# One padded load for the last chunk of W_down, and x in six loads instead of four, in a decode layer on one core

## The chip, the cores and the metric

The kernel runs on one core of one Trainium2 chip. A core has five engines that run their own instruction streams: TensorE (PE: matmuls; PEld: its weight loads), VectorE (DVE), ScalarE (ACT), GpSimd (POOL) and SyncE (SP). Data come from device memory by sixteen DMA engines. A load is issued by SP or by ACT into that issuer's queue, and each of the DMA engines works on its share of the rows. The metric is the device time of one execution in microseconds. Before the change three runs gave 659.60, 659.35 and 658.97; the median is 659.35.

## The reference, cut to what matters

Two tokens (B = 2, one position each) go through a pre-norm attention layer with a key and value cache, and then through a gated feed-forward layer:

```
h  = x + A(layernorm(x))        A: q = n @ wq, 32 heads of 128, 8192 cached positions,
                                   softmax(q k / sqrt(128)) v, then @ wo
h2 = h + Bf(layernorm(h))       Bf: gate = n @ W_gate ; up = n @ W_up
                                    (relu(gate) * up) @ W_down
x [2,1,512]  k_cache, v_cache [2,32,8192,128]  wq [512,4096]  wo [4096,512]
W_gate, W_up [512,1376]  W_down [1376,512]      all bf16
```

The caches make up 268 MB of the 281 MB that are read.

## The kernel before, in words

**The three big buffers.** `bufs[0..2]` hold 64 KB in each of 128 partitions (`TILE` = 32768 bf16 elements). The attention goes through 15 steps of four heads (`steps[0..LASTQ]`, "quad" steps) and two last steps of two heads (p0, p1). The K tile of a quad step is 8 MB and fills one buffer; the V tile is as large. The three buffers are used in turn, in the order K0, V0, K1, V1, K2, ...; a load can only be issued when the tile that was in its buffer has been used up. The V tile of step 1 takes K0's buffer, and goes out when step 0's scores are done; the K tile of step 2 takes V0's buffer, and goes out when step 0's values are done. `bufs[2]` holds wq (4 MB), the row of q and x before K1.

**Order of the work.** All is written out by hand inside `tc.manual_schedule()`: every engine runs its instructions in the order in which they stand. The start is: x (L197 to L200, issued by ACT), then wq, K0 and V0 (L201 to L203, issued by SP). x is transposed on TensorE (L246), normalised (`ln_cols`, L177 to L193), multiplied by wq (L260), and the row of q is spread over the partitions into `qrep` (L272) and `qpair` (L279). Only then is K1 issued (L294), since wq and q lie in its buffer. A step then multiplies K with q on VectorE (`products`, L390), adds up in halves (`scores`, L408, L410), takes the exponentials (L430) and multiplies with V on TensorE (`values`, L461); a part of the scores goes over TensorE (`scores_pe`, L355 to L382).

**The loads' completion counters.** Each load, from whichever queue, gets one of eight completion counters in turn, in the order of the program. A load waits on its issuer until the load eight before it, which had the same counter, has landed, besides waiting for its buffer. SP works through its loads in order, so a load that waits holds those behind it.

**The feed-forward layer.** F = 1376 is not a multiple of 128: ten chunks of 128 rows, and an eleventh that begins at row F - 128 = 1248, so that its first 32 rows are rows that chunk ten already has (`AGAIN` = 32, `FSETS`, `FC` = 11). W_down lies in `wd_sb` as 128 x 11 x 512. Before the change the eleventh chunk is loaded without its first 32 partitions, by three loads of 32 rows (L651 to L654), and VectorE writes zeros into those 32 partitions (L684). Then come four loads with chunks 0 to 4, 5 to 7, 8 and 9 (L655 to L657). W_gate and W_up are read in the same chunks, so gate and up values of the 32 repeated rows exist a second time in the eleventh chunk, and meet the zeros in W_down. The gate is made at L745 for all eleven chunks at once; L766 multiplies it with up, first chunks 0 to 4, then 5 to 10. `down` (L756) then takes chunks 0 to 4, the eleventh, and 5 to 9, and two engines copy the sum to `yrow` (L773, L774), which the last load stores (L775).

Of the kernel before, what the change touches and what calls it, by code (L numbers as in the profile page):

```python
# [13 lines left out]
def _free(t, offset, dims):  # L14

    return bass.AP(tensor=t.tensor, offset=t.offset + offset, ap=[t.ap[0]] + [list(d) for d in dims])


def _dram(t, offset, dims):
    return bass.AP(tensor=t.tensor, offset=t.offset + offset, ap=[list(d) for d in dims])  # L20
# [3 lines left out]
def kernel(  # L24
# [13 lines left out]
    nc = tc.nc  # L38
    P = nc.NUM_PARTITIONS
    B, Sq, D = A_x.shape  # L40
    _, Hkv, Sk, Dh = A_k_cache.shape
    Hq = A_wq.shape[1] // Dh
    F = B_W_gate.shape[1]
# [33 lines left out]
    FSETS = [(0, 5), (5 * P, 3), (8 * P, 1), (9 * P, 1), (F - P, 1)]  # L77
    FC = 11
    AGAIN = 32
# [55 lines left out]
    wd_sb = bufs[1][:, 0:FC * D].rearrange("p (c n) -> p c n", c=FC)  # L135
# [58 lines left out]

    with tc.manual_schedule():

        for b, k, n in ((0, 0, 2), (0, 2, 2), (1, 0, 2), (1, 2, 2)):  # L197
            nc.scalar.dma_start(
                out=xr[b:b + 1, k * P:(k + n) * P], in_=_dram(A_x, b * D + k * P, [[D, 1], [1, n * P]]),
            )  # L200
# [9 lines left out]
            out=nscale, in_=nscale, compare_op=ALU.not_equal, fill=-SCALE,  # L210
# [5 lines left out]
            out=ident_f, in_=ident_f, compare_op=ALU.not_equal, fill=1.0,  # L216
# [4 lines left out]
            out=sel, in_=sel, compare_op=ALU.not_equal, fill=1.0,  # L221
# [9 lines left out]
            out=pick, in_=pick, compare_op=ALU.not_equal, fill=1.0,  # L231
# [24 lines left out]
        for g0 in range(0, NQ, 4):  # L256
            for n0 in range(NH * g0 * Dh, NH * (g0 + 4) * Dh, 4 * Dh):
                q_ps = ps2.tile([B, 4 * Dh], f32, tag="o")
                for c in range(KC):
                    nc.tensor.matmul(  # L260
                        out=q_ps, lhsT=xn[:, c, :], rhs=wq_sb[:, c, n0:n0 + 4 * Dh], start=(c == 0), stop=(c == KC - 1),
                    )
                nc.vector.tensor_copy(qrow[:, n0:n0 + 4 * Dh], q_ps)
            for b in range(B):
                r_ps = ps2.tile([P, 4, Dh], f32, tag="tp")
                for j in range(NH):
                    nc.tensor.matmul(
                        out=r_ps[j * (P // NH):(j + 1) * (P // NH)], lhsT=sel[:, b, 0:P // NH],
# [5 lines left out]
        for j in range(2):  # L274
            nc.tensor.matmul(
                out=r_ps[j * (P // 2):(j + 1) * (P // 2)], lhsT=sel[:, B - 1, :],
# [202 lines left out]
        def values_cols(s, t0, t1):  # L479

            if t0 == 0:
                o_ps[s.i] = ps2.tile([P, 8], f32, tag="o", name="o_ps")
            for t in range(t0, t1):
                nc.tensor.matmul(
                    out=o_ps[s.i][:, 0:2], lhsT=s.vt[:, t * Dh:(t + 1) * Dh],
                    rhs=s.pg[:, t // VG, :, t % VG], start=(t == 0), stop=(t == s.nt - 1),
                )
# [133 lines left out]
        for d0, r, k, m in DEALT:  # L621
            for i in range(m):
                n, at_o = k * PORT, 2 * (d0 > 0) * D
                nc.sync.dma_start(
                    out=wdeal[i * SIDE2:i * SIDE2 + n, at_o:at_o + r * D],
                    in_=_dram(A_wo, (HL * Dh + d0 + i * n * r) * D, [[r * D, k], [k * r * D, PORT], [1, r * D]]),
# [20 lines left out]
        for w, src in ((0, B_W_gate), (1, B_W_up)):  # L647
            nc.sync.dma_start(
                out=wgu[:, w].rearrange("p c f -> p (c f)"), in_=_dram(src, 0, [[KC * F, P], [1, KC * F]]),
            )  # L650
        for q0 in range(AGAIN, P, AGAIN):  # L651
            nc.sync.dma_start(
                out=wd_sb[q0:q0 + AGAIN, FC - 1, :], in_=_dram(B_W_down, (F - P + q0) * D, [[D, AGAIN], [1, D]]),
            )  # L654
        for f0, n in FSETS[:-1]:  # L655
            fc = f0 // P
            nc.sync.dma_start(out=wd_sb[:, fc:fc + n, :], in_=_dram(B_W_down, f0 * D, [[n * D, P], [1, n * D]]))  # L657
        late = bufs[1][:, HALF + D:HALF + D + P + D]
        hrow, parts3 = late[0:3 * B, 0:D], late[0:3 * B, D:D + B]
# [6 lines left out]
            out=z2_ps, lhsT=ones, rhs=_free(zc, ((B - 1) * NQ + groups[Q][1]) * NH, [[1, nb]]), start=True, stop=True,  # L666
# [13 lines left out]
        for k, t1 in ((1, 40), (2, 56), (3, 72)):  # L680
            values_cols(p1, t0, t1)
            lay_rows(k, sps[k - 1]) if k < len(SETS) else lay_dealt()
            t0 = t1
        nc.vector.memset(wd_sb[0:AGAIN, FC - 1, :], 0.0)  # L684
        values_cols(p1, 72, 88)
        sums(Q + 2)
        shares(Q + 2)
# [45 lines left out]
        for c in range(KC):  # L733
            nc.tensor.transpose(hT_ps[:, c, :], hb[:, c].rearrange("p k b -> p (k b)"), ident)
        nc.scalar.activation(
            out=hrow.rearrange("q (p c) -> q p c", c=KC), in_=hT_ps.rearrange("q c p -> q p c"), func=ACT.Copy,
# [7 lines left out]
        gate = small.tile([P, FC, B], f32, tag="gate")  # L744
        nc.vector.scalar_tensor_tensor(  # L745
            out=gate, in0=g_ps, scalar=0.0, in1=_free(rvar, 0, [[0, FC], [1, B]]), op0=ALU.max, op1=ALU.mult,
        )
        parts = [(range(0, UP), "of", ps), (range(UP, FC), "tp", ps2)]
        u_ps = [pool.tile([P, len(part), B], f32, tag=tag, name="u_ps") for part, tag, pool in parts]
        SIDE = P // KC  # L750
# [55 lines left out]
```

## Time and profile before

| | |
|---|---|
| median of three runs | 659.35 us |
| profiled execution | 659.72 us |
| its span, first to last instruction | 657.9 us |
| TensorE busy | 351.5 us (53%) |
| VectorE busy | 558.8 us (85%) |
| ScalarE busy | 123.5 us (19%) |
| GpSimd busy | 8.5 us (1%) |
| moved by DMA | 281.37 MB, 428 GB/s on average |
| mean granted TensorE clock | 0.759 |

The span is the time between the first and the last instruction; 1.8 us of the execution lie around it. Busy shares are averages over the whole span. In timeline rows the columns are start, duration (both us), engine, line, operation, operands and, in brackets, how long the engine had been idle and what ended that. In the chain of work they are start, duration and what ran or was waited for. `tile` stands for any of the three buffers. A queue's row gives its packets, megabytes and the share of the sixteen engines' time.

### The profile page before, as it was taken

To read this page: it belongs to the slowest core of one execution; us is meant where nothing else is said; L and a number is where in the kernel's file an instruction comes from. 1 tells how busy PE (TensorE), PEld (TensorE's weight loads), DVE (VectorE), ACT (ScalarE), POOL (GpSimd) and SP (SyncE) were. 2 spreads that over 40 slices of the span, in tenths; PEclk is the share of its full clock that TensorE was granted. 3 is DMA by queue.
4 is the path that set the end of the run, shared out by engine and by line. 5 is a ranking of instruction groups with operands and counts; after the bars stand their busy time and mean duration, and the time that the engine had idled before them with its cause. 6 is when DMAs were issued, how large, how long until landed. Compare 5 with 4: busy or idle time off the path is not lost.

```text
span 657.9 us, 5149 instructions
## 1 busy us (share of the span) xinstructions
PE 351.5 (53%) x2132; PEld 160.4 (24%) x2132; DVE 558.8 (85%) x256; ACT 123.5 (19%) x337; POOL 8.5 (1%) x34
## 2 busy tenths in 40 slices
PE   1730924709175380926538093562908458291997
PEld 0210311304022130312214031220403224030466
DVE  1499697988979799897979989796997969999982
ACT  1130030301103020030302103030210304201870
POOL 2000000000000000000000000000000000000010
PEclk9975876959679595866959587695967869686885
DMA  9999999999999999999999999999999999999997
GB/s 383 446 443 442 390 447 439 442 434 408 442 438 439 434 415 442 430 446 431 418 442 427 442 438 423 442 427 435 442 427 431 434 431 438 434 424 426 420 423 284
DMA packets 6994, 281.37 MB, mean 428 GB/s; under 512 B 790, under 2 KB 1532, under 8 KB 1980
## 3 DMA queue, kind: packets, MB, share of 16 engines
q1 hardware_dynamic: 6964, 281.06, 99.1%
q8 instruction: 16, 0.26, 0.1%
q14 instruction: 6, 0.05, 0.0%
q10 hardware_dynamic: 8, 0.00, 0.0%
HBM read 281.05 MB, written 0.00 MB: 427 GB/s over the span
## 4 chain that ended last, share of the span: by engine, by line
DVE 42%; DMA 37%; PE 18%; ACT 1%; issue 1%; SPq 0%; ACTq 0%; DVEq 0%
DMA tile<-in_A_k_cache_dram 30%; DVE tile L390 19%; DVE tile L408 18%; PE pv_ps L461 16%; DMA tile<-in_A_wo_dram 4%; DVE scol L410 2%; DMA tile<-in_A_x_dram 2%; DMA tile<-in_B_W_down_dram 1%; PE q_ps L260 1%; DVE pgq L435 1%; ACT ecol L430 1%; DVE pm L414 1%; DVE qrep L410 0%; DVE pm L425 0%; DVE hmax L427 0%
## 5 line engine op out<-in xcount | busy, mean ns | idle before, releaser
L461 PE MATMUL pv_ps<-tile,pgq 128*16 128x512 bf16 x960 | 241.5, 417 | 237.2 <-DVE pgq L435 224.8
L390 DVE TENSOR_TENSOR tile<-tile,qrep 128x29696 bf16<-128x29696 bf16 (+3 forms) x16 | 232.4, 14525 | 46.5 <-DMA tile<-in_A_k_cache_dram 46.5
L408 DVE TENSOR_TENSOR tile<-tile 128x14848 bf16<-128x14848 bf16 (+7 forms) x68 | 236.4, 3477 | 2.2
L461 PEld LDWEIGHTS <-pgq 128*16 128x16 bf16 x960 | 91.1, 97 | 376.9 <-DVE pgq L435 235.4
L365 ACT ACTIVATE tile<-t_ps 128x1024 bf16<-128x1024 bf16 x53 | 52.6, 1022 | 16.2 <-PE t_ps L364 15.8
L466 ACT ACTIVATE pv<-pv_ps 16x512 f32<-16x512 f32 (+1 forms) x16 | 9.4, 588 | 240.9 <-PE pv_ps L461 240.9
L430 ACT ACTIVATE ecol<-scol,nmax 128x256 bf16<-128x256 f32 x14 | 7.1, 507 | 197.4 <-DVE nmax L429 197.4
L364 PE MATMUL t_ps<-ident,tile 128*128 128x128 bf16 x424 | 32.6, 230 | 16.4 <-DMA tile<-in_A_k_cache_dram 16.4
L355 PE MATMUL row_ps<-tile,qz 128*24 128x512 bf16 (+1 forms) x98 | 30.6, 394 | 18.3 <-ACT tile L365 18.2
L364 PEld LDWEIGHTS <-tile 128*128 128x128 bf16 x424 | 26.0, 103 | 31.8 <-DMA tile<-in_A_k_cache_dram 17.2
L410 DVE TENSOR_REDUCE scol<-tile 128x232 f32<-128x1856 bf16 (+1 forms) x14 | 28.9, 2067 | 0.5
L435 DVE TENSOR_TENSOR pgq<-ecol,ownb 128x1024 bf16<-128x1024 bf16 x15 | 10.4, 692 | 10.3 <-ACT ecol L430 10.3
L396 ACT ACTIVATE tile<-tile 128x128 bf16<-128x128 bf16 x60 | 17.6, 294 | 1.9 <-DVE tile L390 1.9
L390 DVE TENSOR_TENSOR tile<-tile,qpair 128x4096 bf16<-128x4096 bf16 (+3 forms) x4 | 15.5, 3883 | 0.0
L355 PEld LDWEIGHTS <-qz 128*24 128x24 bf16 (+1 forms) x98 | 7.9, 93 | 28.3 <-issue 23.3
L382 ACT ACTIVATE scol<-sc_ps 32x24 f32<-32x24 f32 (+1 forms) x56 | 11.7, 209 | 7.7 <-PE sc_ps L377 7.2
L377 PE MATMUL sc_ps<-ident_f,tile 24*128 24x24 f32 (+2 forms) x68 | 7.2, 221 | 11.0 <-ACT tile L373 11.0
L373 ACT ACTIVATE tile<-row_ps 24x512 f32<-24x512 f32 (+2 forms) x17 | 9.9, 585 | 13.5 <-PE row_ps L355 13.5
L396 ACT ACTIVATION_READ_ACCUMULATOR tile<-tile 128x1 f32 x60 | 11.2, 187 | 0.0
L377 PEld LDWEIGHTS sc_ps<-ident_f,tile 24*128 24x128 f32 (+2 forms) x68 | 5.5, 136 | 19.4 <-ACT tile L373 19.4
L247 DVE CAST xc<-x_ps 128x8 f32<-128x8 bf16 x1 | 0.2, 167 | 11.3 <-PE x_ps L246 11.3
L260 PE MATMUL q_ps<-tile,xn 128*2 128x512 bf16 x32 | 9.1, 444 | 1.0 <-DVE xn L193 1.0
(141 smaller groups left out, 135.4 us busy)
## 6 DMA issues: line engine op xcount, KB each, us to landing
tile<-in_A_k_cache_dram SPq DMA_DIRECT2D x2, 4096.0 KB
tile<-in_A_v_cache_dram SPq DMA_DIRECT2D x2, 4096.0 KB, 19.9
tile<-in_A_wq_dram SPq DMA_DIRECT2D x1, 4096.0 KB, 12.3
tile<-in_A_wo_dram SPq DMA_DIRECT2D x1, 2048.0 KB, 24.4
tile<-in_B_W_gate_dram SPq DMA_DIRECT2D x1, 1376.0 KB, 18.0
tile<-in_B_W_up_dram SPq DMA_DIRECT2D x1, 1376.0 KB
tile<-in_A_wo_dram SPq DMA_DIRECT2D x1, 1024.0 KB
tile<-in_B_W_down_dram SPq DMA_DIRECT2D x1, 640.0 KB
```

Of the source, the lines that this page charges most:

```text
L260: nc.tensor.matmul(out=q_ps, lhsT=xn[:, c, :], rhs=wq_sb[:, c, n0:n0 + 4 * Dh], start=(c == 0), stop=(c == KC - 1),)
L355: nc.tensor.matmul(out=row_ps, lhsT=z, rhs=s.kt[:, (nv + c0 + k) * Dh:(nv + c0 + k + 4) * Dh], start=(u == 0), stop=(u == U - 1),)
L364: nc.tensor.transpose(t_ps[:, k, :], s.kt[:, t * Dh:(t + 1) * Dh], ident)
L365: nc.scalar.activation(out=s.kt[:, (nv + c0) * Dh:(nv + c0 + TPC) * Dh], in_=t_ps.rearrange("p t s -> p (t s)"), func=ACT.Copy,)
L377: nc.tensor.transpose(sc_ps[:, t].rearrange("p u j -> p (u j)"), rows[:, t * P:(t + 1) * P], ident_f[0:nh * U, 0:nh * U],)
L390: nc.vector.tensor_tensor(out=kv, in0=kv, in1=_free(s.qr, 0, [[0, n], [1, Dh]]), op=ALU.mult)
L396: nc.scalar.activation(out=kv, in_=kv, func=ACT.Copy, accum_out=scols[s.i][:, t:t + 1])
L408: nc.vector.tensor_tensor(out=lo, in0=lo, in1=hi, op=ALU.add)
L410: nc.vector.tensor_reduce(out=scol[:, s.na:s.nv], in_=_free(s.kt, s.na * Dh, [[Dh, s.nv - s.na], [1, 8]]), axis=AXIS.X, op=ALU.add,)
L430: nc.scalar.activation(out=ecol, in_=scols[s.i], func=ACT.Exp, scale=SCALE, bias=nmax, accum_out=zs[:, s.b, s.g:s.g + 1],)
L435: nc.vector.tensor_tensor(out=s.pg, in0=_free(ecol, 0, [[VG, s.nt // VG], [0, NH], [1, VG]]), in1=_free(ownb, 0, [[0, s.nt // VG], [VG, NH ...
L461: nc.tensor.matmul(out=pv_ps[s.i][r, :], lhsT=s.pg[:, u].rearrange("p j t -> p (j t)"), rhs=s.vt[:, u * VG * Dh:(u + 1) * VG * Dh], start= ...
```

## The change

x, which is one row of 512 elements for each of the two tokens, is loaded in six pieces instead of four: for each token one of 256 elements and two of 128 instead of two of 256. The eleventh chunk of W_down is loaded whole, 128 rows in one load, the first of five from the list `FSETS[-1:] + FSETS[:-1]`; its first 32 partitions now hold the rows that chunk ten has too. The zeros are no longer written into W_down but into the gate values of those 32 partitions, after L745. The number of loads in all stays the same (two more for x, two fewer for W_down); 32 KB more are read. In the changed kernel the lines from L652 on have other numbers.

```diff
-        for b, k, n in ((0, 0, 2), (0, 2, 2), (1, 0, 2), (1, 2, 2)):
+        for b, k, n in ((0, 0, 2), (0, 2, 1), (0, 3, 1), (1, 0, 2), (1, 2, 1), (1, 3, 1)):
             nc.scalar.dma_start(
                 out=xr[b:b + 1, k * P:(k + n) * P], in_=_dram(A_x, b * D + k * P, [[D, 1], [1, n * P]]),
             )
...
-        for q0 in range(AGAIN, P, AGAIN):
-            nc.sync.dma_start(
-                out=wd_sb[q0:q0 + AGAIN, FC - 1, :], in_=_dram(B_W_down, (F - P + q0) * D, [[D, AGAIN], [1, D]]),
-            )
-        for f0, n in FSETS[:-1]:
-            fc = f0 // P
+        for f0, n in FSETS[-1:] + FSETS[:-1]:
+            fc = FC - 1 if f0 == F - P else f0 // P
             nc.sync.dma_start(out=wd_sb[:, fc:fc + n, :], in_=_dram(B_W_down, f0 * D, [[n * D, P], [1, n * D]]))
...
-        nc.vector.memset(wd_sb[0:AGAIN, FC - 1, :], 0.0)
...
+        nc.vector.memset(gate[0:AGAIN, FC - 1, :], 0.0)
```

## The prediction

> **What bounds the kernel now.** First the page's head, its forty slices and its queues, to see whether one resource is full throughout:
>
> ```profile
> span 657.9 us, 5149 instructions
> ...
> DMA  9999999999999999999999999999999999999997
> ...
> q1 hardware_dynamic: 6964, 281.06, 99.1%
> ...
> q10 hardware_dynamic: 8, 0.00, 0.0%
> ```
>
> The sixteen DMA engines are busy in every slice but the last. VectorE (85%) often waits for K, TensorE (53%) for VectorE. So the time is 281 MB at what the engines move, plus each stretch in which an engine has nothing queued, plus what follows the last byte. q1 is SP's queue, with every large load; q10 is ACT's, with x alone: four loads, eight packets, so two each (the data, then the completion count). The chain of work that ended last names the places the change touches:
>
> ```profile
> 1.82 10.70 DMA tile<-in_A_x_dram
> ...
> 28.59 43.74 DMA tile<-in_A_k_cache_dram
> ...
> 644.58 9.73 DMA tile<-in_B_W_down_dram
> 654.31 0.04 issue
> 654.35 0.60 PE d_ps L758 x16
> 654.96 0.03 issue
> 654.99 0.33 PE d_ps L758 x4
> ```
>
> 2 KB of x take 10.7 us. The transfer view in a window from 6 to 7 us (forty bins of 25 ns, GB/s of the packets that start in each) shows why:
>
> ```profile
> GB/s 1311 0 1331 2621 1311 0 0 1311 0 2621 0 0 2621 2621 0 0 0 1311 2621 0 0 0 0 0 0 0 1311 0 0 0 0 0 0 0 0 0 0 0 0 0
> DMA packets 17, 0.52 MB, mean 525 GB/s; under 512 B 0, under 2 KB 1, under 8 KB 1
> ...
> q10 hardware_dynamic: 1, 0.00, 0.2%
> ```
>
> 1311 is one 32 KB row of wq; the 20 over it in the third bin is 512 B of x. The same 20 stands at 8.5 and 10.95 us, the small second packets between. After load one (both packets before 2 us), x gets one packet through for each 1.22 us row of wq: 6.06, 7.3, 8.5, 9.75, 10.95 and 12.18 us. TensorE starts on x at 12.66. The timeline then tells how much room the stages have:
>
> ```profile
> 28.59 0.34 SPq L173 DMA_DIRECT2D tile<-in_A_k_cache_dram  x1
> ...
> 32.42 15.09 DVE L390 TENSOR_TENSOR tile<-tile,qrep 128x28672 bf16<-128x28672 bf16 x1 [1.74 <-DMA tile<-in_A_k_cache_dram]
> ...
> 64.48 0.33 SPq L173 DMA_DIRECT2D tile<-in_A_v_cache_dram  x1
> ...
> 72.45 15.63 DVE L390 TENSOR_TENSOR tile<-tile,qrep 128x29696 bf16<-128x29696 bf16 x1 [5.44 <-DMA tile<-in_A_k_cache_dram]
> ```
>
> VectorE was ready for step 0 at 30.68 and waited 1.74 us for K. Step 1's V load is issued at 64.48, when step 0's scores free K's buffer, 32.06 us after step 0's products start. Between the K load of step 1 and that V load nothing else is queued. The packets where the one ends and the other begins, 69.8 to 72.3 us in bins of 62.5 ns:
>
> ```profile
> GB/s 0 0 0 0 0 0 0 4194 4195 3146 2097 1049 0 0 1049 0 0 0 0 0 0 0 0 0 0 0 0 0 0 0 0 0 0 1049 0 0 0 0 0 0
> ```
>
> The first 64 KB rows of V start on 14 engines from 70.24 to 70.5, on one at 70.7, on one at 71.8. Fifteen engines would run dry if that load arrived after about 70.5.
>
> **The change part by part.** *x in six loads.* Twelve packets instead of eight, on the same engine. The first eight fall as before, to 12.18 us. There wq ends: its own count lets packet nine through at once, and ten, eleven and twelve each wait for a row of K, which is 64 KB. From their first starts (12.2 to 12.7) to the count packets (31.1 to 32.0) eight rows take 19.3 us, so 2.41 each. The last packet goes at 12.18 + 3 x 2.41 = 19.4, TensorE starts at 19.9: x is 7.24 us later. Bounds: two rows (4.8 us) if x gets in one turn earlier at the start, four (9.65 us) if wq's last row and its count make one turn. I take three, since x's own counts had turns of their own.
>
> The Trainium skill, page "DMA: Bandwidth & Descriptors", section "Queues, rings and completion order", says that an engine switches between queues only after a whole packet, typically 9 to 17 descriptors. With K's eight rows and count as one packet, x would wait for whole tiles, three times about 19 us. Here wq gave x a turn after each row, so the trace speaks for one row a turn.
>
> What hangs on x (transposes, norm, wq, q's copies) moves whole by 7.24: nothing in it waits for another load, wq having landed at 13.0. Step 1's K load goes out at 28.59 + 7.24 = 35.8, covered by V of step 0, whose rows run to about 51. VectorE is ready at 30.68 + 7.24 = 37.92, so step 0 starts 5.5 us late; 1.74 us of its wait is the cover used up. The V load of step 1 moves to 64.48 + 5.5 = 69.98. From an issue to its first packets the nearest row is wq's at the start: 0.74 to 1.73 us, so 0.99. The rows arrive at 70.97: a gap of 0.27 to 0.73 us on fifteen engines, none on the sixteenth. Refilling costs more: after the start wq's first row was followed by its second after 1.85 us instead of 1.22, 0.63 lost. Loss per engine: from 0 (the late engine decides the end) to 0.73 + 0.63 = 1.36. I take 1.36, because the counts show the late engine changing along the run (at 109 to 111 us two lag, at 553 to 557 all sixteen are spread over 3 us), so the engine that ends last is most likely one that lost.
>
> Next in line is step 2's K load, issued at 82.92 when step 0's values are done: 88.4, its rows at 89.4, while V's rows now end at 89.5 + 1.0 or more: covered. VectorE ends step 0 at 67.01 + 5.5 = 72.5, level with the K it waits for (72.45), so its 5.44 us of idle time is gone but step 1 starts on time, and from step 2 on all is as before, later by the gap. 281 MB at a full rate leave no place to win that back.
>
> *Waits of the loads.* Completion counters go round by eight, so a load waits for the one eight before it. The V load of step 0 now waits on SP for the first x load (both packets out by 2 us): from 1.64 to about 2.5. Behind it on SP is only step 1's K load; 4 + 8 MB stand in the queue until 31 us. Nothing. The two more issues on ACT (213 to 506 ns each) push its table load, which ends at 3.4, by at most 1 us, against x at 19.9. Nothing. Later loads keep the same partners, the total being the same.
>
> *W_down's tail.* Three loads of 32 rows (issues of 0.34, 0.31 and 0.42 us) become one. The last of W_down's loads waited 2.5 us for W_gate and went out at 647.91; it now waits for a piece of W_o that had landed, and goes at about 644.5 before the shift. Each engine gets eight 1 KB rows and one count for six rows and three counts; the packets of 654.0 to 654.5 (34 in 17.4% of 16 engines, 0.5 us) cost 0.041 us each, so the change is 0. By bytes alone 32 KB at 428 GB/s are +0.08, which I take; below, the earlier issue could gain at most 0.4, since the 20 matmuls after 654.35 could then follow the 24 before them without the wait. *Memsets.* Gone is 0.27 us at 642.35, ahead of a wait for TensorE of 0.52; new is a 32 x 2 fill (L240's 128 x 1 took 0.06) between these:
>
> ```profile
> 651.51 0.18 DVE L745 SCALAR_TENSOR_TENSOR gate<-g_ps,rvar 128x22 f32<-128x22 f32 x1
> ...
> 652.62 0.17 DVE L766 TENSOR_TENSOR hm<-gate,u_ps 128x10 bf16<-128x10 f32 x1 [0.92 <-PE u_ps L725]
> ```
>
> It lies in 0.92 us of waiting for TensorE, which waits for W_up. Without that cover it would cost 0.06 to 0.1.
>
> Sum: 1.36 + 0.08 = +1.4. The profiled execution took 659.72 (span 657.9 and 1.8 around it), so 661.1; the median of the three runs is 659.35, 0.37 lower, so 660.8 there.
>
> **The rivals.** *Four turns.* x is 9.65 later, step 0 starts 7.9 late, V goes out at 72.4 and arrives at 73.4: gaps of 2.7 to 3.1, 0.63 for the refill, 0.08: +3.4 to +3.8, 663.0. For it: a row and its count may be one turn. Against: x's two packets were not.
>
> *Hidden.* Two turns: step 0 starts 3.1 late, V arrives at 68.6, in time; or the sixteenth engine stays the last. +0.1, 659.4. For it: the gap is smaller than the uncertainty of one turn. It decides from any x later than about 6.5 us.
>
> *Faster.* Each load may cost its engines a dead time. The lone output load takes 1.96 us from its issue (655.94) to the end of the span, for 2 KB. If all of that were dead, two fewer would save 3.9 in the tail, against the 1.4 lost at the start: 656.9. From 1.35 us dead per load on, the kernel is faster by over 0.2%: 658.0. Against it: from 640 to 650 us, where those loads were queued, the engines are 100% busy or more. The Trainium skill, same page, section "Anatomy of one DMA — SWDGE (gpsimd) path", gives about 2.0 us fixed per load; by that alone the sum would be 4 us lower. It describes another issuing path, and in this trace one load's latency lies under the next one's rows.
>
> **How the numbers follow.** The likeliest case, three turns, 0.48; four or more, 0.27; hidden, 0.13; faster, 0.12. 0.2% is 1.3 us, about what a measurement of this kernel can tell from no change. The first case lies across it: two thirds above (0.32), as its gap is a lower bound if issue takes longer on a busy queue. Slower 0.32 + 0.27 = 0.59, same 0.16 + 0.13 = 0.29, faster 0.12. The range runs from 659.0 (hidden, less 0.4 for the tail) to 663.4 (four turns); outside are the faster case and a little above. The likeliest alone: 659.4 to 661.0.
>
> **What would show it.** Twelve packets on q10; TensorE's first transposes at 19.9 (17.5 or 22.3 with another turn); the second K load at 35.8; VectorE's first products at 37.9 without a wait for K; V at 70.0 and a hole after the rows of K; products of step 2 at 112.3 instead of 111.02. A start of x before 18.5 makes the prediction wrong, as does an end of W_down's loads that moves by more than the hole.

## The result, and the profile after

The changed kernel takes 661.4 us in the median (660.99 to 662.28) against 659.25 us before: ratio 1.0035, 95% interval 1.0022 to 1.0048. It is slower by about 2.2 us, on the side that was forecast; the forecast was 660.8. The likeliest case alone was given as 659.4 to 661.0, so 661.4 lies a little above it and inside the whole range. The profiled execution took 660.99 us, with a span of 659.2. One execution below, the profiled one of late_7us, ran at a much lower clock (0.55, span 720.8 us) and is left out.

The page of the changed kernel, head, slices and queues:

```profile
span 659.2 us, 5150 instructions
...
DMA  9999999999999999999999999999999999999997
...
q1 hardware_dynamic: 6964, 281.09, 98.9%
...
q10 hardware_dynamic: 12, 0.00, 0.0%
```

The queues are nearly as busy as before (98.9% for 99.1%), 0.03 MB more are moved, and x takes twelve packets instead of eight. Where the loss arises can't be seen on this page. The chain of work that ended last (start, duration, what) shows where it begins and that the tail is not the place:

```profile
2.40 17.48 DMA tile<-in_A_x_dram
...
36.08 36.47 DMA tile<-in_A_k_cache_dram
...
645.97 10.25 DMA tile<-in_B_W_down_dram
656.22 0.04 issue
656.26 0.33 PE d_ps L754 x4
```

x takes 17.5 us instead of 10.7, and step 1's K load is issued 7.5 us later, but lands when it did. The timeline of the changed kernel, in start, duration, engine and line, with the wait in brackets:

```profile
70.16 0.33 SPq L173 DMA_DIRECT2D tile<-in_A_v_cache_dram  x1
...
38.11 15.08 DVE L390 TENSOR_TENSOR tile<-tile,qrep 128x28672 bf16<-128x28672 bf16 x1
72.63 15.62 DVE L390 TENSOR_TENSOR tile<-tile,qrep 128x29696 bf16<-128x29696 bf16 x1
112.83 15.62 DVE L390 TENSOR_TENSOR tile<-tile,qrep 128x29696 bf16<-128x29696 bf16 x1 [4.59 <-DMA tile<-in_A_k_cache_dram]
```

Steps 0, 1 and 2 start at 38.11, 72.63 and 112.83 us, before at 32.42, 72.45 and 111.02. Step 1 is on time, although the waits for K ahead of steps 0 and 1 are gone; step 2 is 1.81 us late, since its K stands in the queue behind the V load issued at 70.16. The packets of the changed kernel from 69.8 to 72.3 us, in bins of 62.5 ns:

```profile
GB/s 0 0 0 0 0 0 0 0 0 0 0 0 0 0 0 0 0 0 0 0 1049 3146 2097 3146 0 0 1049 1049 2097 0 1049 0 0 1049 0 0 0 0 1049 0
```

Before, V's first rows started as K's last ones ended, most of them from 70.24 to 70.5. Now nothing starts before 71.05, and the sixteen starts spread to 72.2: the hole that the prediction described. Fifteen engines ended K between 70.23 and 70.61 in this run; the sixteenth had a row of K until 72.22.

### The profile page after: what moved, and what is told of

The parts are those of the page before. It is cut to its first block, busy times and chain, and to the rows that moved or that the text cites. A ratio compares the mean times of both kernels' runs of the same rounds, so it can differ in the third digit from the quotient of the medians.

```text
span 659.2 us, 5150 instructions
## 1 busy us (share of the span) xinstructions
PE 350.5 (53%) x2132; PEld 159.0 (24%) x2132; DVE 558.4 (85%) x256; ACT 123.7 (19%) x337; POOL 8.9 (1%) x34
## 3 DMA queue, kind: packets, MB, share of 16 engines
q1 hardware_dynamic: 6964, 281.09, 98.9%
## 4 chain that ended last, share of the span: by engine, by line
DVE 42%; DMA 37%; PE 18%; ACT 1%; issue 1%; SPq 0%; ACTq 0%; DVEq 0%
DMA tile<-in_A_k_cache_dram 30%; DVE tile L390 19%; DVE tile L408 18%; PE pv_ps L461 16%; DMA tile<-in_A_wo_dram 4%; DMA tile<-in_A_x_dram 3%; DVE scol L410 2%; DMA tile<-in_B_W_down_dram 2%; PE q_ps L260 1%; DVE pgq L435 1%; ACT ecol L430 1%; DVE pm L414 1%; DVE qrep L410 0%; DVE pm L425 0%; DVE hmax L427 0%
```

## The experiments

Times are set against the kernel before, on the same chip. "V issued" is the issue of step 1's V load in the profiled execution.

| run | x starts | step 0 starts | V issued | step 2 starts | median us | before us | ratio, 95% interval |
|---|---|---|---|---|---|---|---|
| before | 12.66 | 32.42 | 64.48 | 111.02 | | | |
| changed | 20.02 | 38.11 | 70.16 | 112.83 | 661.40 | 659.25 | 1.0035, 1.0022 to 1.0048 |
| x6_only | 20.22 | 38.56 | 70.60 | 113.16 | 662.02 | 659.32 | 1.0035, 1.0022 to 1.0049 |
| tail_only | 12.92 | 32.38 | 64.44 | 111.01 | 659.15 | 659.32 | 0.9997, 0.9988 to 1.0006 |
| x5_loads | 15.04 | 32.90 | 64.94 | 110.88 | 659.45 | 659.32 | 1.0001, 0.9992 to 1.0010 |
| x7_loads | 24.85 | 42.74 | 74.78 | 117.28 | 667.08 | 659.32 | 1.0117, 1.0103 to 1.0130 |
| late_5us | 12.79 | 37.91 | 69.91 | 113.12 | 661.45 | 659.42 | 1.0027, 1.0018 to 1.0037 |
| late_7us | | | | | 665.13 | 659.42 | 1.0082, 1.0065 to 1.0098 |
| late_9 | 12.79 | 37.15 | 69.14 | 111.85 | 660.37 | 659.29 | 1.0014, 1.0005 to 1.0023 |
| six_cut | 20.07 | 37.94 | 64.48 | 110.83 | 659.10 | 659.42 | 0.9992, 0.9983 to 1.0000 |
| six_on_sp | 13.72 | 32.35 | 64.41 | 111.13 | 658.98 | 659.29 | 0.9995, 0.9986 to 1.0005 |
| x2_tail | 7.94 | 32.34 | 64.39 | 110.92 | 659.34 | 659.42 | 0.9995, 0.9986 to 1.0004 |

**One part alone.** x6_only is the kernel before with the change's first line; tail_only is the changed kernel with that line undone.

```diff
-        for b, k, n in ((0, 0, 2), (0, 2, 2), (1, 0, 2), (1, 2, 2)):
+        for b, k, n in ((0, 0, 2), (0, 2, 1), (0, 3, 1), (1, 0, 2), (1, 2, 1), (1, 3, 1)):
```

> x in six loads, W_down's tail as before. Theory (x late, step 0 late, fifteen DMA engines run dry ahead of step 1's V load): all of the loss is here, ratio 1.0020 to 1.0035 to the kernel before; first transposes of x at 20.0 us, V load of step 1 issued at 70.1, products of step 2 at 112 to 113 instead of 111.0. Rival (the tail in one load costs the time): 1.000, although x comes just as late.

> x in four loads as before, W_down's eleventh chunk in one load of 128 rows with the gate zeroed. Theory: no change, ratio 0.9995 to 1.0005 (+0.1 us for 32 KB at most, -0.4 at best). Rival (the tail costs or each small load has dead time): 1.002 to 1.0035 if the padded load is what costs, 0.994 to 0.998 if two fewer loads save dead time.

x6_only lost what the whole change lost, tail_only nothing: 1.0035 and 0.9997, with intervals far apart. All of the loss belongs to x; neither 32 KB more, nor two loads fewer, nor the filled gate values can be measured. In the changed kernel the new fill stands in the timeline of VectorE where it was expected, in the shadow of a wait for TensorE:

```profile
652.82 0.18 DVE L740 SCALAR_TENSOR_TENSOR gate<-g_ps,rvar 128x22 f32<-128x22 f32 x1
653.05 0.06 DVE L743 MEMSET gate<- 32x2 f32 x1
653.72 0.17 DVE L762 TENSOR_TENSOR hm<-gate,u_ps 128x10 bf16<-128x10 f32 x1 [0.61 <-PE u_ps L720]
```

**Less and more of the same.** Five and seven loads of x, all else as before.

```diff
-        for b, k, n in ((0, 0, 2), (0, 2, 2), (1, 0, 2), (1, 2, 2)):
+        for b, k, n in ((0, 0, 2), (0, 2, 2), (1, 0, 2), (1, 2, 1), (1, 3, 1)):
...
+        for b, k, n in ((0, 0, 2), (0, 2, 1), (0, 3, 1), (1, 0, 1), (1, 1, 1), (1, 2, 1), (1, 3, 1)):
```

> The kernel before with x in five loads (the last 256 elements of the second token in two). Ten packets: the ninth goes as wq ends, the tenth after one row of K, so x is 2.4 us later, first transposes at 15.1 us; VectorE starts step 0 at 33.1, 0.7 us late, the V load of step 1 goes out at 65.2 and comes in time. Theory (a threshold: x may be 6.5 us late for nothing): 1.000. Rival (every delay of x is paid in full or in part, since the kernel is at the DMA limit): 1.001 to 1.0037.

> The kernel before with x in seven loads (a 256 and two 128 for the first token, four 128 for the second). Fourteen packets, five rows of K after wq: x is 12.1 us later, first transposes at 24.7; step 0 starts 10.3 to 10.5 us late, the V load of step 1 goes out at 74.9, its rows at 75.8, a hole of 5.1 to 5.5 us on fifteen engines, about 4 on the sixteenth, plus 0.6 to refill. Theory: +5.5 to +6.1 us over the kernel before, ratio 1.0085 to 1.0095. Rival (x's packets or the two queues' sharing cost by themselves, some 1 us for each load more): +3 to +4 us.

The starts of x came out as worked out: 15.04 (15.1 expected) and 24.85 (24.7). The fifth load cost nothing. The seventh cost 7.7 us by the ratio, more than the 5.5 to 6.1 expected, and far from the rival's +3 to +4. So the delay is free up to a point and is then paid about in full. At step 2 the seven loads are 6.26 us late, close to the upper end expected. The profiled execution, the quickest of the four, ends 6.7 us after the one before (spans 664.6 and 657.9), so only some 0.4 us of it arises after step 2; the rest of the 7.7 is what the other executions took longer than the profiled one.

**The delay without x.** Here x and all loads are those of the kernel before, and VectorE is held up by itself ahead of step 0 (11 times in late_5us, 16 in late_7us, 9 in late_9).

```diff
+        for _ in range(11):
+            nc.vector.memset(pv, 0.0)
         place_q(steps[0])
```

> The same with 11 fills: step 0 starts at 36.0, 3.6 us late, the V load of step 1 goes out at 68.1 and its rows can start at 69.0, ahead of the first engine's need at 70.24. Theory: 1.000. Rival (a later step 0 costs in proportion, some 60% of late_7us): 1.0015 to 1.0025.

> The kernel before, x and W_down's loads untouched; VectorE fills the scratch tile pv with zeros 16 more times (0.48 us each) ahead of step 0's products, which so start at 38.4 instead of 32.4 us. Theory (only step 0's lateness counts, through the V load of step 1): that load goes out at 70.4, rows start at 71.3 and later, products of step 2 at 112.8 to 113.3, ratio 1.0025 to 1.0042, the same loss as with six loads of x. Rival (x's packets, the V load of step 0 waiting for x, or the later K load cost it): 1.000, as none of these is changed.

A fill took 0.66 us and not 0.48, as each waited 0.17 us for the one before it. So late_5us started step 0 at 37.91 and issued V at 69.91, where the changed kernel has 38.11 and 70.16, and the run that had been meant to lose nothing became a near copy: 1.0027 (1.0018 to 1.0037) against 1.0035. x on time, its eight packets and the K load of step 1 issued at 28.77 did not help. The timeline of late_5us:

```profile
69.91 0.33 SPq L173 DMA_DIRECT2D tile<-in_A_v_cache_dram  x1
...
37.51 0.48 DVE L546 MEMSET pv<- 128x512 f32 x1 [0.17 <-DVE pv L546]
37.91 15.03 DVE L390 TENSOR_TENSOR tile<-tile,qrep 128x28672 bf16<-128x28672 bf16 x1
...
113.12 15.63 DVE L390 TENSOR_TENSOR tile<-tile,qrep 128x29696 bf16<-128x29696 bf16 x1 [5.16 <-DMA tile<-in_A_k_cache_dram]
```

Step 2 waits for K until 113.12, as long as with six loads of x. late_7us gained another 3.3 us of delay (five fills) and lost 3.6 us more: 1.0082, where 1.0025 to 1.0042 had been expected for a shorter delay. It has no stage times in the table; by an estimate, five fills on top of late_5us put its V load at 73.2.

The reverse takes the same step away from the changed kernel. Six loads of x, but VectorE has less to do in step 0:

```diff
+            self.skip = 40 if i == 0 else 0
...
-            products(s)
+            products(s, s.skip)
+            if i == 0:
+                nc.vector.memset(scols[0][:, 0:s.skip], 0.0)
```

> The changed kernel with six loads of x, whose step 0 leaves out 40 of the 224 position groups that VectorE scores (their scores are set to 0), which takes 5.7 us off its 31.9. x comes at 20.0 us as in the changed kernel, step 0 starts at 38.1, the V load of step 1 goes out at 64.5 again. Theory: the loss is gone, 1.000 to the kernel before. Rival (the late x or the later K load costs in another place too): 1.0015 to 1.0035 stays.

x comes at 20.07 and K of step 1 is issued at 35.85, both as late as in the changed kernel, but V is issued at 64.48 again, and the loss is gone (0.9992). Its timeline, where one line more ahead of these shifts the numbers by one:

```profile
35.85 0.33 SPq L174 DMA_DIRECT2D tile<-in_A_k_cache_dram  x1
64.48 0.33 SPq L174 DMA_DIRECT2D tile<-in_A_v_cache_dram  x1
...
37.94 12.41 DVE L391 TENSOR_TENSOR tile<-tile,qrep 128x23552 bf16<-128x23552 bf16 x1
72.23 15.63 DVE L391 TENSOR_TENSOR tile<-tile,qrep 128x29696 bf16<-128x29696 bf16 x1 [5.22 <-DMA tile<-in_A_k_cache_dram]
110.83 15.63 DVE L391 TENSOR_TENSOR tile<-tile,qrep 128x29696 bf16<-128x29696 bf16 x1 [2.99 <-DMA tile<-in_A_k_cache_dram]
```

The products of step 0 are 2.7 us shorter (12.41 for 15.08), the sums after them by as much again, and step 1's wait for K is back. Put together: late x with V on time loses nothing; x on time with V late loses all.

**The way x takes.** The same six loads, issued by SP behind wq:

```diff
-            nc.scalar.dma_start(
+            nc.sync.dma_start(
                 out=xr[b:b + 1, k * P:(k + n) * P], in_=_dram(A_x, b * D + k * P, [[D, 1], [1, n * P]]),
             )
```

> The changed kernel with its six loads of x issued by SP, behind wq in the same queue, instead of by ACT in a queue of their own. Same loads, same bytes. Theory (x loses turns only because two queues take turns on the DMA engine): all twelve packets follow wq's rows at about 12.2 us, first transposes at 12.7 to 13.2, the V load of step 1 at 64.5, no loss: 1.000 to the kernel before, although K of step 0 is issued some 2 us later. Rival (six loads cost by their number): first transposes at 18 or later, 1.002 to 1.0035.

TensorE started on x at 13.72, a little later than expected, and nothing was lost (0.9995). Six loads do not cost; six loads in a queue that takes turns with 32 and 64 KB rows do.

**A candidate.**

> x in two loads of 512 elements and W_down's eleventh chunk in one load. Four packets: first transposes at about 7.8 us, then q waits for wq at 13.0, so step 1's K load goes out some 3 us earlier than in the kernel before, step 0 still waits for K at 32.4. Theory: no change against the kernel before, 0.9995 to 1.0005, the DMA queues being full from there on. Rival (an earlier start of q is worth something): 0.995 to 0.998.

x came at 7.94 and step 1's K load went out at 26.25, and nothing was gained: 0.9995, an interval that holds 1. No version was found that is clearly faster than the kernel before.

**Where the threshold lies.** The losses by the ratios, taken from the issue times of V, give nearly one number: 69.91 less 1.8, 70.16 less 2.3, 70.60 less 2.3 and 73.2 less 5.4 are 68.1, 67.9, 68.3 and 67.8. Seven loads (74.78 less 7.7) give 67.1. Each loss has an interval of about a microsecond to either side or less; the delays of step 2 in the traces, from 0.83 us in late_9 to 6.26 with seven loads, give 67.8 to 68.5 for all five runs that have one. The prediction's hole opens only for an issue after 69.25 (70.24 less the 0.99 us from issue to rows). One more run between the two:

> The kernel before with 9 of the zero fills, which took 0.66 us each in late_5us. Step 0 starts at 36.6, the V load of step 1 goes out at 68.6, its first rows can start at 69.5, before the first engine is through with K at 70.24. Theory as predicted (a hole opens only when rows come later than 70.24): 1.000. Rival (the engines need the load some 1.5 us ahead, as the losses of late_5us, the changed kernel and x6_only point to a threshold at an issue of about 68.0): +0.5 to +0.9 us, 1.0007 to 1.0014.

Its V load went out at 69.14, somewhat later than planned, with rows ready at 70.1. It lost 0.9 us (1.0014, 1.0005 to 1.0023): the rival's side, and 69.14 less 0.9 is 68.2 once more (its interval reaches from 0.3 to 1.5 us). The packets of late_9 from 69.8 to 72.3 us:

```profile
GB/s 0 0 0 0 1049 0 3146 3146 3146 2097 0 0 1049 0 0 0 0 0 0 1049 0 0 1049 0 0 0 0 0 0 0 0 0 0 0 0 0 0 0 0 1049
```

There is no hole for thirteen engines: their first rows of V start from 70.05 to 70.6, as soon as in the kernel before. Two more start at 71.0 and 71.2, after a gap, and the sixteenth still had a row of K. What is missing on the thirteen shows one row later. From 72 to 75 us, in bins of 75 ns, the kernel before and then late_9:

```profile
GB/s 0 0 0 0 0 0 0 0 1748 5243 2621 1748 874 0 874 0 0 0 0 0 0 0 0 0 0 0 0 0 0 0 0 874 0 0 0 0 0 0 0 0
```

```profile
GB/s 0 0 0 874 0 0 0 0 0 0 0 0 0 0 0 874 874 2621 3495 874 1748 0 874 874 0 0 0 0 0 0 874 0 0 0 0 874 0 0 0 0
```

The second rows start from 72.6 to 73.1 before and mostly from 73.1 to 73.8 in late_9. So the first row of a load that reaches an engine at the last moment takes longer, with hardly a gap ahead of it: by the packet records 2.8 to 3.4 us on the thirteen engines, 3.1 on the average, where each of these first rows took 2.42 before. An engine needs its next load some time before it is through with the last row.

How long before is known only between bounds. The 68.0 above, 2.2 us ahead of the first engine's need at 70.24, is where the losses point if each microsecond of delay costs one; no run issued that load between 64.94 (no loss) and 69.14 (0.9 us). Step 2's K loads, in the same traces, narrow it. In the changed kernel that load goes out at 89.56, 1.41 us before the first engine ends V (its count packet is at 90.97), and its first rows take 0.12 us longer on the average; with seven loads, 1.72 us ahead, it is 0.04, and in late_9, 2.41 us ahead, 0.18. In late_9 the V load went out 0.94 us ahead (first count at 70.08), and the sixteen first rows took 0.61 us longer on the average. So most of that cost is gone when the load is issued 1.4 us ahead.

## Why the prediction was right or wrong, point by point

- **x's three rows of K: right.** TensorE started on x at 20.02; 19.9 was forecast. After wq's end packets of x fell at 14.7, 17.1 and 19.5 us, one per row. Five and seven loads follow the same count. Two readings are slightly off: K's first count packets stand at 31.39 us and not 31.1, and V's last first row at 71.9 and not 71.8; the 2.41 us per row come out of the right ones too.
- **One turn per row: shown.** The runs with five, six and seven loads give steps of 2.4 to 5 us, one or two rows for a load. By the typical packet size of 9 to 17 descriptors in the Trainium skill, page "DMA: Bandwidth & Descriptors", section "Queues, rings and completion order", taken with a row as one descriptor, x would have come after whole tiles. The runs disagree with that, and here the measurement decides; how many descriptors a row is, no trace shows.
- **From x to the V load: right.** Step 1's K load at 36.08 (35.8), step 0 at 38.11 (37.9), V at 70.16 (70.0), each covered or passed on as written. That this one issue carries the loss is shown by late_5us and six_cut.
- **The hole: right in kind, too small.** The term "0.73 + 0.63 = 1.36" was the one mis-sized. Step 2 measured +1.81 in the profiled execution (112.83, where 112.3 was forecast) and the whole change 2.3 us by the ratio. Two things were off. One issue-to-rows time of 0.99 had been used for all engines: the first row did come 0.95 us after the issue, but on the fifteen engines that had run dry the starts spread from 71.11 to 71.87, so the gaps were about 0.9 to 1.25 us where 0.27 to 0.73 was forecast. The trace before had that spread already, in wq's first rows (1.75 to 2.49). And the 0.63 was added only behind a gap, where late_9 shows it with hardly any, so the loss began earlier than at the 6.5 us of delay given for x: late_9's V load, at 69.14, stands for 6.4 us and lost 0.9, and the losses together point to some 5.3 us (V issued at 68.0).
- **From step 2 to the end: not exact.** "Later by the gap" fits the medians (661.4 and 659.25). The two profiled executions end only 1.3 us apart (spans 657.9 and 659.2), 0.5 us less than at step 2; where that went wasn't traced.
- **The late sixteenth engine: right.** V's load of step 1 ended only 0.4 us later on its last engine (last count packet 91.31 before, 91.72 after), but 1.6 us later in the middle of the sixteen (89.78, 91.37). The next load, K of step 2, ended 1.7 us later on its last engine (110.63, 112.37), as one or two engines were again over a microsecond behind in both traces. The traces show what makes an engine late: a 16 KB packet of queue q8, "instruction", took one engine for 0.93 to 0.96 us (at 36.64 and 92.25 before, at 44.01 and 101.30 after), and the row behind it 2.9 us instead of 2.42. The second of these fell on another engine, during the load in question, in both runs, so the late engine was then one that had lost like the others.
- **Waits of the loads: right.** V of step 0 went out at 1.98 instead of 1.64 (2.5 was forecast), without effect.
- **The tail and the memsets: right that they cost nothing.** The +0.08 for 32 KB is below what tail_only can measure (0.9997). W_down's last load went out at 646.0 instead of 647.91, and that gained nothing either.
- **The rivals.** Four turns: out, x came at 20.02. Hidden: out for six loads, true for five. Faster by dead time per load: out, as tail_only's interval ends at -0.8 us. By an estimate from the fixed time of about 2.0 us per load in the Trainium skill, page "DMA: Bandwidth & Descriptors", section "Anatomy of one DMA — SWDGE (gpsimd) path", which is about another way of issuing, two loads fewer would have saved some 4 us. In this tail, where other rows are queued, it doesn't add up.
- **What stays open:** why a first row takes longer when its load comes late, and how far ahead of 69.14 the V load must go out to lose nothing.

## What to carry to other kernels

Here a small load in a queue of its own paid one row of the big loads for each of its packets, and each piece has two (data and count), so a piece more costs up to two of the neighbour's rows; put it behind the big load in the same queue or make it one piece. In a kernel that keeps its DMA engines full, look for the issue with the least room ahead of the moment when the queue runs dry: delays are free until there, and are paid in full from there on. Count that room not to the end of the last row but to some 1.5 to 2 us before it: in these runs a load issued 0.94 us ahead lost time, and one issued 1.4 us ahead nearly none.

## What the runs showed of the hardware that was not expected

A load that arrives just in time still costs: in late_9 thirteen engines had hardly a gap, and their second rows still started some 0.6 us later than before. A 16 KB packet of the instruction queue puts one of the sixteen engines about 1.4 us behind the others (0.93 to 0.96 us for itself, some 0.5 in the row after it), and a load is complete only when that engine is through. Fills of the same buffer back to back (128 x 512, f32) started 0.66 us apart though each ran for 0.48, with 0.17 us of waiting for the fill before.
